# Weights' sign by a slope on ScalarE, and one pass of lane sums instead of two, in a planned attention and feed-forward kernel

## The chip, the cores and the metric

The kernel runs on one core of one Trainium2 chip. The metric is device time in microseconds (us) of one execution; 0.5% of it, about 3.2 us, is what a measurement of this kernel can tell from no change.

## The reference, cut to what matters

```
q, k, v: 4 batches x 12 heads x 448 x 64, float32          cap = 30
scores = cap * tanh(q k^T / 8 / cap);  attn = softmax(scores);  a = attn v
x = heads of a side by side                                  # 1792 x 768
h = relu(x @ w_in);  g = s * h * h + b;  out = g @ w_out     # 768 -> 2048 -> 768
```

`w_in` and `w_out` reach the chip as float64, 8 bytes an element; the rest is float32. [...]

## The kernel before

**A planner writes the order.** The kernel is a list of operations, each with an engine (or several that could run it), a cost in microseconds, a rank, and the buffers that it reads and writes. `Plan.emit` runs through a clock of its own: each engine takes, of the operations that are ready, the one with the smallest rank. What it lays down is the fixed instruction order of every engine, SyncE's order of DMA issues included. `bias`, `shy`, `cling` and `late` in `CHOICE` weight that choice. Operations are grouped in units, and `CHOICE['at']` gives each unit its rank and a step by which its parts are spread: `('a', b, c)` is the attention of two pairs of heads (c and c+1) of batch b, `('w', g)` one of 8 groups of columns of `w_in`, `('o', d)` one of 6 groups of columns of `w_out`, `('p', p)` a mixture of two of these, `('m1', j, f)` and `('m2', j, d)` the first and second product of batch j. `arrange` sorts the units by rank (no unit before those it needs); buffers of one pool are given out in that order.

**Attention.** For one pair of heads, `scores` makes 3 chunks of 128 keys (and, for every second pair, one chunk of the last 64 keys of two pairs) in the PSUM tile `ps_s` (two buffers), and ScalarE applies Tanh (L516) and Exp (L520) to 128x896 each. `pv` multiplies these with V on TensorE (`value`, L570) and adds them over the keys (`total`, L578) in the one buffer of `ps_v`: the row sums come from `ones`, twice, over chunks 0 and 1 in a first round and over chunk 2 and the last chunk in a second. A round is 8 matmul instructions of the trace. ScalarE takes `ps_v` out to `pw` (L598). `normal` moves the sums by DMA to a 128x7 tile, adds two rows and a guard on GpSimd (L541, L542), inverts them on VectorE (L545), and brings the inverse back by two more DMAs.

**Loads.** `load` issues K and Q of a pair at its rank less 10, V somewhat later; the first pair of all has a rank written out by hand:

```
        if bb == c2 == 0:
            rank = -90
        kr = buf(("k", bb, c2), "kraw", [128, S], F32)
        dma(229376, rank - 10, lambda: nc.sync.dma_start(P[kr], kT[bb, c2]), w=[kr])
        ...
        dma(
            262144, vrank - 10,
```

`vrank` is the unit's rank + 0.73 of its step, and is not written out by hand. The cap value, which ScalarE and VectorE need before the first Tanh, is loaded at rank -100 too. `piece` loads 512 KB of weights at rank - 8; `win` passes it the unit's rank + 2c for its 3 pieces. Groups 0 and 1 (`alias` is 2) are loaded into the memory of `gt`, which is idle at first, so they wait for no buffer.

**Weights.** A piece is 128 x 512 float64, seen as pairs of 32-bit words. VectorE shifts the low word (L662) and puts the sign into it (L663); the high word, read as float32, is multiplied by 2^-112 on VectorE or GpSimd (L434, L436), which sets the exponent; VectorE joins the two (L666). There are 48 pieces, 24 of each matrix. `win` then squares them, sums the squares on TensorE (L712), and derives the scales in small steps (L720 to L733), one of which waits for a sum over lanes on TensorE (L477).

**Products.** `m1` and `m1pair` multiply x with the parts of `w_in` (L843 to L845), `m2` and `m2pair` the activations with `w_out` (L1094 to L1096, L1003).

Of the kernel before, what the change touches and what calls it, by code (L numbers as in the profile page):

```python
# [243 lines left out]
def arrange(units, at):  # L244

    key = {}
    for name, pre, _ in units:
# [4 lines left out]
CHOICE = {  # L252
    'bias': 1.806,
    'shy': {'DVE': 0.3, 'POOL': 0.5},
# [32 lines left out]
    },  # L287
    'alias': 2,
    'direct': 6,
    'cslag': 21,  # L290
    'late': 0.621,
    'lag': 0.0,
    'cling': 19.274,
    'parts': ((0, 1), (2, 3)),
    'warm': 6,
    'pvo': 0.73,
    'ahead': 0.3,
    'tail': 0.9,
    'evac': ('ACT',),
    'sq': ('ACT', 'DVE', 'POOL'),  # L300
    'expo': ('DVE', 'POOL'),
    'whi': ('ACT', 'DVE'),
# [13 lines left out]
    'cs': ('DVE', 'POOL'),  # L316
    'fast': (2, 3),
    'slots': (
        ('w', 7), ('kraw', 3), ('qraw', 3), ('vp', 3), ('ph', 5), ('pt', 2), ('rd', 3), ('pw', 3),
# [6 lines left out]
def attention_moe_kernel(  # L326
# [13 lines left out]
    nc = tc.nc  # L340
# [126 lines left out]
    def root2(p):  # L467
        pi = p.bitcast(I32)
        nc.vector.tensor_scalar(pi, pi, EXP, 1, ALU.bitwise_and, ALU.logical_shift_right)
        nc.vector.tensor_scalar(pi, pi, 127 << 22, None, ALU.add)  # L470
        nc.vector.tensor_scalar(pi, pi, EXP, None, ALU.bitwise_and)
# [51 lines left out]
    def normal(bb, c2, rank):  # L523
# [15 lines left out]
        def whole():  # L539
            a = P[kc][:, 0]  # L540
            nc.gpsimd.tensor_tensor(a, a, P[kc][:, 1], ALU.add)  # L541
            nc.gpsimd.tensor_scalar(a, a, guard[:, 0:1], 0.0, ALU.add, ALU.add)  # L542

        gps(0.55, rank, whole, r=["guard", *((kc, h, i) for h in range(2) for i in range(2))], w=[kc], port=True)
        dve(0.32, rank, lambda: nc.vector.reciprocal(P[kc][:, 0], P[kc][:, 0]), w=[kc])  # L545
        z = zd[bb * NP + c2]
# [13 lines left out]
    def pv(bb, c2, rank, step):  # L560
# [11 lines left out]
        def total(first, last):  # L572
            for h, i, o in quarter:
                if i and last:
                    w, ph = half[:, c2 % 2], prob(NC, h)
                else:
                    w, ph = ones[:, 0:32], prob(i if first else 2, h)
                nc.tensor.matmul(P[kp][o, 1, 0:S], w, ph, start=first, stop=last)  # L578

        for part in CHOICE["parts"]:  # L580
            both = part[0] == 0

            def run(part=part, both=both):
                for c in part:
                    value(c)
                if both:
                    total(True, False)
                if part[-1] == NC:
                    total(False, True)

            n = len(part) + both + (part[-1] == NC)
            pe(
                0.75 * n, rank + part[-1] * step, run, r=[*(kh[c] for c in part), *(kh[0:2] if both else ()), kv, "one"],
                w=[kp], kind=2,
            )
        kw = buf(("pw", bb, c2), "pw", [128, 2, S], F32)
        ways = {
# [17 lines left out]
        def gather():  # L615
# [5 lines left out]
            gather,  # L621
            r=[("xm", bb, c) for c in range(NP)], w=[("xn", bb)], port=True,
        )
# [23 lines left out]
    def piece(kr, src, n, rank, over=()):  # L647
# [12 lines left out]

        def sign():
            nc.vector.tensor_scalar(lo(), lo(), 29, None, ALU.logical_shift_right)  # L662
            nc.vector.scalar_tensor_tensor(lo(), hi(), -0x80000000, lo(), ALU.bitwise_and, ALU.bitwise_or)  # L663

        def join():
            nc.vector.scalar_tensor_tensor(hi(), hi(), 3, lo(), ALU.logical_shift_left, ALU.bitwise_or)  # L666

        dve(0.25 + n * 0.0018, rank, sign, r=[kr], w=[(kr, "s")], port=True)
        scaled(CHOICE["expo"], n, rank, hf, hf, 2.0 ** -112, [(kr, "s")], [kr])
        dve(0.07 + n * 0.0011, rank + 0.5, join, r=[kr, (kr, "s")], w=[(kr, "f")], port=True)  # L670
        return hf
# [14 lines left out]
    def win(g, rank):  # L686
# [38 lines left out]
        kl = lanes(("wps", g), rank, g, [("wnm", g)])  # L725

        def fin():
            nc.vector.tensor_copy(n[:, 1:2], P[kl][:, 0:1])
            root2(n)
            nc.vector.reciprocal(ip, n)  # L730
            nc.vector.tensor_tensor(wn[:, g:g + 1], n[:, 0:1], n[:, 0:1], ALU.mult)
            nc.vector.tensor_scalar(sw, ip[:, 1:2], 8192.0, None, ALU.mult)
            nc.vector.tensor_scalar(wc[:, g:g + 1], ip[:, 0:1], n[:, 1:2], 1.0 / 2097152.0, ALU.mult, ALU.mult)  # L733

        dve(1.75, rank, fin, r=[kl], w=[("wnm", g), ("wc", g)], port=True)
        for c in range(NC3):
# [13 lines left out]
    def wout(d, rank):  # L750
# [44 lines left out]
        def amax():  # L795
# [4 lines left out]
        dve(  # L800
            0.68, rank, amax, r=[("wc", g) for g in range(NG)] + [("om", d, q) for q in range(NQ)], w=[("om", d)],
            port=True,
        )
# [5 lines left out]

        dve(1.3, rank, fin, r=[kl], w=[("op", d), ("os", d)], port=True)  # L810
        half = NQ // 2
# [380 lines left out]
    for d in range(ND):  # L1192
        put(("o", d), [("w", NG - 1)], lambda rank, step, d=d: wout(d, rank))
    for p in range(ND // 2):
        put(("p", p), [("o", 2 * p), ("o", 2 * p + 1)], lambda rank, step, p=p: mix(p, rank, step))
    m2s = []
    for j in range(B):
        m1s, fast = [], j in CHOICE["fast"]
        for f in range(NG if fast else NF):
            g = f if fast else f // 2  # L1200
            pre = [("a", j, NP - 2), ("w", g), ("w", CHOICE["alias"] - 1), *m2s]
            one = m1pair if fast else m1
            put(("m1", j, f), pre, lambda rank, step, j=j, f=f, one=one: one(j, f, rank))
            m1s.append(("m1", j, f))
# [60 lines left out]
```

## Time and profile before

| | |
|---|---|
| median of 3 runs | 640.17 us (638.66 to 641.72) |
| the profiled execution | 639.61 us, of which the span of the trace is 637.8 us |
| TensorE busy | 627.0 us, 98% of the span |
| VectorE / ScalarE / GpSimd busy | 400.2 / 351.7 / 208.1 us |

The span runs from the first to the last instruction of the core; what lies around it is 1.8 us. Busy time counts instructions in progress; TensorE's matmuls overlap, so its lines are read by the distance from one start to the next. PE is TensorE, PEld its weight loads, DVE VectorE, ACT ScalarE, POOL GpSimd, and SPq the DMA issues of SyncE.

### The profile page before, as it was taken

How to read it: one execution, taken by the hardware profiler on the slowest of the kernel's cores; microseconds unless marked ns; L12 is line 12 of the kernel's file. 1: busy time of each engine (PE TensorE's matmuls, PEld its weight loads, DVE VectorE, ACT ScalarE, POOL GpSimd, SP SyncE). 2: the span in 40 equal slices, each digit the busy share in tenths (PEclk: the TensorE clock that was granted, in tenths of full speed). 3: DMA queues.
4: the chain of work that ended last, by engine and by line, in shares of the span. 5: the costliest groups of instructions: out<-in, count | busy, mean ns of one | idle time of the engine just before them, and what ended most of it. 6: DMA issues, size and time to landing. Idle time of an engine off the chain costs nothing.

```text
span 637.8 us, 11435 instructions
## 1 busy us (share of the span) xinstructions
PE 627.0 (98%) x4404; PEld 331.4 (52%) x4404; DVE 400.2 (63%) x810; ACT 351.7 (55%) x472; POOL 208.1 (33%) x238
## 2 busy tenths in 40 slices
PE   7999899999999999999999999999999999999997
PEld 2332344344444433434454445555558996556997
DVE  5986857888797878788773341577767222537322
ACT  5889787886884585684674531346354002445100
POOL 3343511546456544466151020117643000105000
PEclk9999899999999999999999999999999999999999
DMA  8766423654262775853854013385412774001671
GB/s 301 293 184 193 124 86 107 215 175 143 60 234 59 251 211 179 272 200 92 282 195 157 1 48 128 146 280 212 164 48 89 239 260 147 1 2 53 223 256 67
DMA packets 54774, 101.67 MB, mean 159 GB/s; under 512 B 16192, under 2 KB 34752, under 8 KB 54720
## 3 DMA queue, kind: packets, MB, share of 16 engines
q1 hardware_dynamic: 54720, 100.95, 48.2%
q8 instruction: 34, 0.56, 0.4%
q14 instruction: 20, 0.16, 0.1%
HBM read 82.58 MB, written 18.17 MB: 158 GB/s over the span
## 4 chain that ended last, share of the span: by engine, by line
PE 85%; DMA 8%; DVE 3%; ACT 1%; SPq 1%; POOL 1%; issue 0%; ACTq 0%
PE ps_v L570 9%; PE ps_m L1003 9%; PE ps_s L512 7%; PE ps_s L1003 6%; PE ps_m L843 6%; PE ps_s L844 6%; PE ps_m L844 6%; PE ps_s L843 6%; PE ps_m L845 6%; PE ps_s L845 6%; PE ps_m L1094 5%; PE ps_m L1095 5%; PE ps_m L1096 5%; PE ps_v L578 4%; DMA gt<-in_w_in 2%; DMA w<-in_w_out 2%
## 5 line engine op out<-in xcount | busy, mean ns | idle before, releaser
L1003 PEld LDWEIGHTS <-w 128*128 128x128 f16 x1008 | 96.6, 98 | 1.0
L516 ACT ACTIVATE bed<-ps_s,arena 128x896 f32<-128x896 f32 x84 | 81.5, 1006 | 9.9 <-PE ps_s L512 8.2
L520 ACT ACTIVATE bed<-bed,par 128x896 f32<-128x896 f32 x84 | 84.2, 1040 | 0.2
L570 PE MATMUL ps_v<-bed 128*32 128x448 f32 x768 | 83.0, 548 | 0.8 <-ACT pw L598 0.6
L512 PE MATMUL ps_s<-bed 64*128 64x448 f32 (+1 forms) x384 | 80.6, 578 | 1.9 <-DMA bed<-in_qT 1.6
L1094 PE MATMUL ps_m<-gt,w 128*128 128x448 f16 x192 | 67.7, 353 | 0.0
L843 PE MATMUL ps_m<-x,w 128*128 128x448 f16 x192 | 67.7, 353 | 0.0
L1096 PE MATMUL ps_m<-gt,w 128*128 128x448 f16 x192 | 67.7, 353 | 0.0
L844 PE MATMUL ps_s<-x,w 128*128 128x448 f16 x192 | 67.7, 353 | 0.0
L844 PE MATMUL ps_m<-x,w 128*128 128x448 f16 x192 | 67.7, 353 | 0.0
L845 PE MATMUL ps_m<-x,w 128*128 128x448 f16 x192 | 67.7, 353 | 0.0
L843 PE MATMUL ps_s<-x,w 128*128 128x448 f16 x192 | 67.7, 353 | 0.0
L1095 PE MATMUL ps_m<-gt,w 128*128 128x448 f16 x192 | 67.7, 352 | 0.0
L845 PE MATMUL ps_s<-x,w 128*128 128x448 f16 x192 | 67.7, 352 | 0.0
L843 PEld LDWEIGHTS <-w 128*128 128x128 f16 x384 | 37.5, 98 | 37.3 <-issue 2.1
L845 PEld LDWEIGHTS <-w 128*128 128x128 f16 x384 | 37.5, 98 | 35.0
L844 PEld LDWEIGHTS <-w 128*128 128x128 f16 x384 | 37.6, 98 | 33.8
L512 PEld LDWEIGHTS ps_s<-bed 64*128 64x128 f32 (+1 forms) x384 | 27.4, 177 | 43.5 <-issue 12.2
L938 ACT ACTIVATE pw<-ps_s,arena 128x448 f32<-128x448 f32 x32 | 20.1, 632 | 52.6 <-PE ps_s L845 49.7
L570 PEld LDWEIGHTS ps_v<-bed 128*32 128x32 f32 x768 | 20.3, 109 | 51.4 <-issue 35.7
L444 POOL TENSOR_TENSOR pw<-pw 128x224 f32<-128x224 f32 x24 | 21.6, 912 | 77.6 <-ACT pw L942 71.2
L578 PE MATMUL ps_v<-bed,ones 128*32 128x448 f32 x288 | 45.5, 545 | 0.0
(142 smaller groups left out, 1012.8 us busy)
## 6 DMA issues: line engine op xcount, KB each, us to landing
w<-w SPq DMA_DIRECT2D x48, 512.0 KB, 4.9
w<-in_w_out SPq DMA_DIRECT2D x24, 512.0 KB, 5.0
w<-ws SPq DMA_DIRECT2D x24, 512.0 KB, 4.9
w<-in_w_in SPq DMA_DIRECT2D x18, 512.0 KB, 5.5
bed<-in_v SPq DMA_DIRECT2D x24, 256.0 KB, 4.2
ws<-w SPq DMA_DIRECT2D x12, 512.0 KB, 2.9
bed<-in_kT SPq DMA_DIRECT2D x24, 224.0 KB, 3.3
bed<-in_qT SPq DMA_DIRECT2D x24, 224.0 KB, 3.6
```

The lines of the kernel that those rows point to most:

```text
L512: nc.tensor.matmul(P[kp][o, h, 0:S], keys, P[q][rows], start=True, stop=True)
L516: 1.01, rank, lambda: nc.scalar.activation(P[kh], P[kp][:, :, 0:S], AF.Tanh, scale=tsc[:, 0:1]),
L520: 1.04, rank, lambda: nc.scalar.activation(P[kh], P[kh], AF.Exp, scale=par[:, 0:1]), r=["par"], w=[kh],
L570: nc.tensor.matmul(P[kp][o, 0, 0:S], P[kv][:, c, o], prob(c, h), start=(c == 0), stop=(c == NC))
L578: nc.tensor.matmul(P[kp][o, 1, 0:S], w, ph, start=first, stop=last)
L843: nc.tensor.matmul(ps[:, 0:S], wh, x[:, 0], start=(c == 0), stop=False)
L844: nc.tensor.matmul(ps[:, 0:S], wh, x[:, 1], start=False, stop=False)
L845: nc.tensor.matmul(ps[:, 0:S], wl, x[:, 0], start=False, stop=(c == NP - 1))
L1003: nc.tensor.matmul(at(), w(g, zw), b(g, zb), start=g == 0 and x == 0, stop=g == n - 1 and x == 2,)
L1094: nc.tensor.matmul(ps[:, 0:S], wh, ghi[:, f], start=(f == 0), stop=False)
L1095: nc.tensor.matmul(ps[:, 0:S], wh, glo[:, f], start=False, stop=False)
L1096: nc.tensor.matmul(ps[:, 0:S], wl, ghi[:, f], start=False, stop=(f == NF - 1))
```

## The change

- **Sign.** The pass that puts the sign into the low word goes. The scaling of the high word becomes a Prelu on ScalarE (scale 2^-112, slope 2^32 for negative values, which leaves a mark in the exponent that the join shifts into the sign), or two passes on VectorE; GpSimd no longer does it. The shift of the low word no longer stands before it.
- **Lane sums.** For batches 2 and 3 the exponentials of chunks 1 and 2 are added onto chunk 0, on VectorE or GpSimd, once `value` has read it, and `total` runs once, over this sum and the last chunk.
- **Small steps.** The two GpSimd steps of `normal` become one on VectorE; in `win` the part of the scales that needs no sum over lanes is made ahead of it (`own`); some steps no longer count as sharing a port in the planner, and `o` units wait for all `w` units in the sort.
- **Ranks.** All ranks and steps of `at` are others, and so are `bias`, `late` and `cling`; so the planner lays down another order on every engine.

```
-    'bias': 1.806,
+    'bias': 3.969,
...
-        ('a', 0, 0): (-88.4, 62.61), ('a', 0, 2): (80.2, 2.4), ('a', 0, 4): (227.3, 40.55),
+        ('a', 0, 0): (-48828.5, 66.74), ('a', 0, 2): (117.1, 0.11), ('a', 0, 4): (366.1, 8.16),
...
-        ('w', 0): (58.5, 0.01), ('w', 1): (226.3, 0.01), ('w', 2): (-88.5, 0.01), ('w', 3): (581.8, 0.01),
-        ('w', 4): (227.6, 0.01), ('w', 5): (510.6, 0.02), ('w', 6): (813.9, 0.02), ('w', 7): (602.1, 0.01),
+        ('w', 0): (-1550585.6, 0.0), ('w', 1): (-7883742.6, 0.02), ('w', 2): (120.7, 0.0), ('w', 3): (43.2, 0.0),
+        ('w', 4): (464.0, 0.0), ('w', 5): (707.7, 0.1), ('w', 6): (1094.7, 0.01), ('w', 7): (760.5, 0.0),
...
-    'late': 0.621,
+    'late': 0.05,
-    'cling': 19.274,
+    'cling': 13.813,
+    'expo': ('ACT', 'DVE'),
-    'expo': ('DVE', 'POOL'),
+    'added': (2, 3),
+    'add': ('DVE', 'POOL'),
...
         def whole():
             a = P[kc][:, 0]
-            nc.gpsimd.tensor_tensor(a, a, P[kc][:, 1], ALU.add)
-            nc.gpsimd.tensor_scalar(a, a, guard[:, 0:1], 0.0, ALU.add, ALU.add)
+            nc.vector.scalar_tensor_tensor(a, a, guard[:, 0:1], P[kc][:, 1], ALU.add, ALU.add)
+            nc.vector.reciprocal(a, a)
...
-                    w, ph = ones[:, 0:32], prob(i if first else 2, h)
+                    w, ph = ones[:, 0:32], prob(i if first else 0 if added else 2, h)
...
+            if part[0] == 0 and added:
+                for c in range(1, NC):
+                    flat = lambda c: P[kh[c]].rearrange("p a b -> p (a b)")
+                    binary(
+                        CHOICE["add"], 2 * S, rank + part[-1] * step, lambda: flat(0), lambda: flat(0),
+                        lambda c=c: flat(c), ALU.add, [kh[c]], [kh[0]],
+                    )
+        if added:
+            pe(0.75, rank + NC * step, lambda: total(True, True), r=[kh[0], kh[NC], "one"], w=[kp], kind=2)
...
-        def sign():
+        def low():
             nc.vector.tensor_scalar(lo(), lo(), 29, None, ALU.logical_shift_right)
-            nc.vector.scalar_tensor_tensor(lo(), hi(), -0x80000000, lo(), ALU.bitwise_and, ALU.bitwise_or)
...
+        def two():
+            nc.vector.tensor_scalar(hf(), hf(), 2.0 ** -112, None, ALU.mult)
+            nc.vector.scalar_tensor_tensor(hf(), hf(), 2.0 ** 32, hf(), ALU.mult, ALU.min)
...
+                lambda: nc.scalar.activation(hf(), hf(), AF.Prelu, scale=2.0 ** -112, alpha=2.0 ** 32),
...
+        def own():
+            root2(n[:, 0:1])
+            nc.vector.reciprocal(ip[:, 0:1], n[:, 0:1])
+            nc.vector.tensor_scalar(wn[:, g:g + 1], n[:, 0:1], n[:, 0:1], None, ALU.mult)
```

## Rows read from the trace of the kernel before

**Rows 1.** The page's busy time, share of the span and instructions, by engine
```profile
PE 627.0 (98%) x4404; PEld 331.4 (52%) x4404; DVE 400.2 (63%) x810; ACT 351.7 (55%) x472; POOL 208.1 (33%) x238
```

**Rows 2.** Windows: stretch; busy PE, PEld, DVE, ACT, POOL; clock; DMA share; GB/s
```profile
0.00:5.00 5.00, 2.42 (x6) 0.74 (x6) 0.38 (x3) 1.49 (x2) 1.34 (x11) 1.00 0.49 137
5.00:12.40 7.40, 6.00 (x22) 2.13 (x23) 4.60 (x8) 4.77 (x5) 1.96 (x2) 1.00 0.98 374
12.40:85.00 72.60, 69.86 (x580) 22.36 (x580) 58.53 (x126) 65.06 (x75) 30.20 (x36) 0.98 0.63 199
85.00:360.00 275.00, 274.19 (x1843) 118.49 (x1842) 206.38 (x447) 188.74 (x249) 118.13 (x139) 1.00 0.51 168
360.00:637.80 277.80, 274.53 (x1961) 187.71 (x1959) 130.30 (x228) 91.60 (x144) 56.48 (x51) 1.00 0.41 136
```

**Rows 3.** Timeline of TensorE: start, length, what, idle before it and releaser
```profile
5.10 4.12 PE L512 MATMUL ps_s<-bed 64*128 64x448 f32 x12 [0.60 <-DMA bed<-in_qT]
...
11.49 0.97 PE L512 MATMUL ps_s<-bed 64*64 64x448 f32 x4 [0.96 <-DMA bed<-in_qT]
...
68.54 0.35 PE L712 MATMUL ps_m<-ones,bed 128*128 128x1 bf16 x8 [1.66 <-DVE bed L701]
```

**Rows 4.** Timeline of SyncE's DMA issues at the start
```profile
1.18 0.42 SPq L488 DMA_DIRECT2D bed<-in_kT  x1
1.64 0.42 SPq L490 DMA_DIRECT2D bed<-in_qT  x1
2.11 1.39 SPq L654 DMA_DIRECT2D w<-in_w_in  x3
3.54 0.61 SPq L488 DMA_DIRECT2D bed<-in_kT  x1
...
6.17 1.82 SPq L494 DMA_DIRECT2D bed<-in_v  x2
```

**Rows 5.** Timeline of TensorE in the attention of a later batch
```profile
246.77 1.71 PE L570 MATMUL ps_v<-bed 128*32 128x448 f32 x16
248.30 0.94 PE L578 MATMUL ps_v<-bed,ones 128*32 128x448 f32 x8
249.16 1.77 PE L512 MATMUL ps_s<-bed 64*128 64x448 f32 x8
```

**Rows 6.** Groups of instructions by line: count | busy us, mean ns | idle before
```profile
L520 ACT ACTIVATE bed<-bed,par 128x896 f32<-128x896 f32 x84 | 84.2, 1040 | 0.2
L516 ACT ACTIVATE bed<-ps_s,arena 128x896 f32<-128x896 f32 x84 | 81.5, 1006 | 9.9 <-PE ps_s L512 8.2 <-PE ps_v L578 1.6
...
L663 DVE SCALAR_TENSOR_TENSOR w<-w 128x512 int32<-128x512 int32 x42 | 38.0, 906 | 1.4
...
L436 POOL TENSOR_SCALAR w<-w 128x512 f32<-128x512 f32 x34 | 27.9, 824 | 34.9 <-DVE w L663 23.1 <-issue 2.6 <-DVE arena L728 2.5
...
L598 ACT ACTIVATE pw<-ps_v 128x896 f32<-128x896 f32 x24 | 21.9, 914 | 12.3 <-PE ps_v L578 7.2 <-issue 3.6 <-POOL cmp L542 0.7
...
L542 POOL TENSOR_SCALAR cmp<-cmp,arena 128x7 f32<-128x7 f32 x24 | 14.6, 607 | 2.4
...
L444 POOL TENSOR_TENSOR w<-bed,w 128x1024 f16<-128x1024 f32 x5 | 11.0, 2205 | 57.6 <-ACT w L918 57.6
L541 POOL TENSOR_TENSOR cmp<-cmp 128x7 f32<-128x7 f32 x24 | 9.9, 412 | 41.7 <-DMA cmp<-pw 33.7 <-DVE arena L470 7.9
...
L443 DVE TENSOR_TENSOR w<-bed,w 128x1024 f16<-128x1024 f32 x7 | 8.5, 1231 | 4.3 <-ACT w L918 4.3
...
L700 ACT ACTIVATE bed<-w 128x512 bf16<-128x512 f32 x6 | 4.1, 688 | 1.3 <-DVE w L666 1.3
...
L1153 ACT ACT_TABLE_LOAD x1 | 1.3, 1283 | 0.7 <-PEq L1255 0.7
```

More of the change, by code (lines that the diff above doesn't have):

```diff
@@ L540, in whole @@
             a = P[kc][:, 0]
-            nc.gpsimd.tensor_tensor(a, a, P[kc][:, 1], ALU.add)
-            nc.gpsimd.tensor_scalar(a, a, guard[:, 0:1], 0.0, ALU.add, ALU.add)
-        gps(0.55, rank, whole, r=["guard", *((kc, h, i) for h in range(2) for i in range(2))], w=[kc], port=True)
-        dve(0.32, rank, lambda: nc.vector.reciprocal(P[kc][:, 0], P[kc][:, 0]), w=[kc])
+            nc.vector.scalar_tensor_tensor(a, a, guard[:, 0:1], P[kc][:, 1], ALU.add, ALU.add)
+            nc.vector.reciprocal(a, a)
+        dve(
+            0.38, rank, whole, r=["guard", *((kc, h, i) for h in range(2) for i in range(2))], w=[kc], port=True,
+        )
         z = zd[bb * NP + c2]
@@ L576, in total @@
                 else:
-                    w, ph = ones[:, 0:32], prob(i if first else 2, h)
+                    w, ph = ones[:, 0:32], prob(i if first else 0 if added else 2, h)
                 nc.tensor.matmul(P[kp][o, 1, 0:S], w, ph, start=first, stop=last)
+        added = bb in CHOICE["added"]
         for part in CHOICE["parts"]:
-            both = part[0] == 0
+            both = part[0] == 0 and not added
             def run(part=part, both=both):
@@ L587, in run @@
                     total(True, False)
-                if part[-1] == NC:
+                if part[-1] == NC and not added:
                     total(False, True)
-            n = len(part) + both + (part[-1] == NC)
+            n = len(part) + both + (part[-1] == NC and not added)
             pe(
@@ L595, in pv @@
             )
+            if part[0] == 0 and added:
[4 more added lines that the diff above has]
+                        lambda c=c: flat(c), ALU.add, [kh[c]], [kh[0]],
+                    )
+        if added:
+            pe(0.75, rank + NC * step, lambda: total(True, True), r=[kh[0], kh[NC], "one"], w=[kp], kind=2)
         kw = buf(("pw", bb, c2), "pw", [128, 2, S], F32)
@@ L621, in pv @@
             gather,
-            r=[("xm", bb, c) for c in range(NP)], w=[("xn", bb)], port=True,
+            r=[("xm", bb, c) for c in range(NP)], w=[("xn", bb)],
         )
@@ L659, in piece @@
         hf = lambda: P[kr].bitcast(F32)[:, :, 1]
-        def sign():
+        def low():
             nc.vector.tensor_scalar(lo(), lo(), 29, None, ALU.logical_shift_right)
-            nc.vector.scalar_tensor_tensor(lo(), hi(), -0x80000000, lo(), ALU.bitwise_and, ALU.bitwise_or)
         def join():
             nc.vector.scalar_tensor_tensor(hi(), hi(), 3, lo(), ALU.logical_shift_left, ALU.bitwise_or)
-        dve(0.25 + n * 0.0018, rank, sign, r=[kr], w=[(kr, "s")], port=True)
-        scaled(CHOICE["expo"], n, rank, hf, hf, 2.0 ** -112, [(kr, "s")], [kr])
-        dve(0.07 + n * 0.0011, rank + 0.5, join, r=[kr, (kr, "s")], w=[(kr, "f")], port=True)
+        def two():
+            nc.vector.tensor_scalar(hf(), hf(), 2.0 ** -112, None, ALU.mult)
+            nc.vector.scalar_tensor_tensor(hf(), hf(), 2.0 ** 32, hf(), ALU.mult, ALU.min)
+        ways = {
+            "ACT": (
+                0.29 + n * 0.00084,
+                lambda: nc.scalar.activation(hf(), hf(), AF.Prelu, scale=2.0 ** -112, alpha=2.0 ** 32),
+            ),
+            "DVE": (0.36 + n * 0.00158, two),
+        }
+        P.any({e: ways[e] for e in engines(CHOICE["expo"])}, rank, [kr], [(kr, "h")], port=True)
+        dve(0.16 + n * 0.00052, rank, low, r=[kr], w=[(kr, "s")], port=True)
+        dve(0.07 + n * 0.0011, rank + 0.5, join, r=[kr, (kr, "s"), (kr, "h")], w=[(kr, "f")], port=True)
         return hf
@@ L725, in win @@
         kl = lanes(("wps", g), rank, g, [("wnm", g)])
+        def own():
+            root2(n[:, 0:1])
+            nc.vector.reciprocal(ip[:, 0:1], n[:, 0:1])
+            nc.vector.tensor_scalar(wn[:, g:g + 1], n[:, 0:1], n[:, 0:1], None, ALU.mult)
+        dve(0.85, rank + 0.1, own, r=[("wnm", g)], w=[("wnm", g, 0)])
         def fin():
             nc.vector.tensor_copy(n[:, 1:2], P[kl][:, 0:1])
-            root2(n)
-            nc.vector.reciprocal(ip, n)
-            nc.vector.tensor_tensor(wn[:, g:g + 1], n[:, 0:1], n[:, 0:1], ALU.mult)
+            root2(n[:, 1:2])
+            nc.vector.reciprocal(ip[:, 1:2], n[:, 1:2])
             nc.vector.tensor_scalar(sw, ip[:, 1:2], 8192.0, None, ALU.mult)
             nc.vector.tensor_scalar(wc[:, g:g + 1], ip[:, 0:1], n[:, 1:2], 1.0 / 2097152.0, ALU.mult, ALU.mult)
-        dve(1.75, rank, fin, r=[kl], w=[("wnm", g), ("wc", g)], port=True)
+        dve(1.5, rank, fin, r=[kl, ("wnm", g, 0)], w=[("wnm", g), ("wc", g)])
         for c in range(NC3):
@@ L800, in wout @@
         dve(
-            0.68, rank, amax, r=[("wc", g) for g in range(NG)] + [("om", d, q) for q in range(NQ)], w=[("om", d)],
-            port=True,
+            0.68, rank, amax, r=[("wc", g) for g in range(NG)] + [("om", d, q) for q in range(NQ)], w=[("om", d)]
         )
@@ L808, in fin @@
             nc.vector.tensor_scalar(sc, wn, si, None, ALU.mult)
-        dve(1.3, rank, fin, r=[kl], w=[("op", d), ("os", d)], port=True)
+        dve(1.3, rank, fin, r=[kl], w=[("op", d), ("os", d)])
         half = NQ // 2
@@ L1192, in attention_moe_kernel @@
     for d in range(ND):
-        put(("o", d), [("w", NG - 1)], lambda rank, step, d=d: wout(d, rank))
+        put(("o", d), [("w", g) for g in range(NG)], lambda rank, step, d=d: wout(d, rank))
     for p in range(ND // 2):
@@ L1200, in attention_moe_kernel @@
             g = f if fast else f // 2
-            pre = [("a", j, NP - 2), ("w", g), ("w", CHOICE["alias"] - 1), *m2s]
+            pre = [("a", j, NP - 2), ("w", g), *(("w", a) for a in range(CHOICE["alias"])), *m2s]
             one = m1pair if fast else m1
```

56 rows, old and new, of the table CHOICE are left out of this document.

## Prediction

> **What bounds the kernel now.** I read the page's busy times first [rows 1], then the same by stretches [rows 2], then TensorE's timeline where it waits [rows 3], the DMA issues at the start [rows 4], one pair of heads in detail [rows 5], and the groups by line for prices [rows 6]. The reader is to see that TensorE is the bound nearly everywhere: 627.0 of 637.8 us. The idle 10.8 us lie at the ends: stretch by stretch [rows 2], 3.98 us before 12.4, 2.74 us up to 85, 0.81 us up to 360, and 3.27 us after, which is the tail of the last product. So relief for VectorE, ScalarE or GpSimd can give back 3.6 us of idle time in the middle at the very most, plus what the clock lost (mean 0.98 of full over 72.6 us, 1.45 us). Two things can move the time by more: the amount of work on TensorE, and the moment at which it starts. The change touches both.
>
> ScalarE is the second bound, in the early stretch alone: 65.06 of 72.6 us [rows 2]. A pair of heads has 3.5 chunks of Tanh and Exp and one copy out: 3.5 x (1.006 + 1.040) + 0.914 = 8.1 us [rows 6].
>
> **Lane sums: less work on TensorE.** 12 pairs (6 in each of batches 2 and 3) lose one round of 8 matmuls, 96 of 4404. In [rows 5], 16 matmuls of the same form take 248.30 - 246.77 = 1.53 us from start to start, so 8 take 0.765 us; the round with the switch to another form takes 249.16 - 248.30 = 0.86 us. Where the single round now stands by itself behind other work, a switch of 0.86 - 0.765 = 0.10 us comes back. Bounds: 12 x 0.665 = 8.0 us and 12 x 0.86 = 10.3 us; I take 12 x 0.765 = **-9.2 us**, since the first round sits between neighbours that stay. All of it counts, because TensorE has no slack to hide it in.
>
> The adds: 24 of 128x896. No add of this shape and type is in the trace. The nearest rows are the 128x1024 ones [rows 6], 1.231 us on VectorE and 2.205 us on GpSimd; by 896/1024 that is 1.08 and 1.93 us. So 26 us on VectorE, or 46 us on GpSimd, which was busy 208 of 638 us. Both adds of a pair run one behind the other, 2.2 us or 3.9 us, between `value` of chunk 0 and `total`; `value` of chunks 2 and 3 (1.53 us) and scores of the next pair (1.7 us) stand there as cover [rows 5], and products of earlier batches besides. With that I cost them at nothing. Without it every us that the chain sticks out keeps `ps_v`, which has one buffer, from the next pair, 12 us in all.
>
> **Sign.** The pass that goes costs VectorE 0.906 us (38.0 us for 42 of the 48 pieces), and GpSimd's scaling 27.9 us for 34 [rows 6]. A Prelu of 128x512 is not in the trace; the nearest is ScalarE's Square of 128x512, 0.688 us; the bounds are that and twice the VectorE pass, 1.8 us, for the two passes there. VectorE comes out near 400 - 43 + 26 + 5 = 388 us, and ScalarE at 352 to 385 us. None of these is the bound, so the sum gets **0**, with the middle's 3.6 + 1.45 us as the most that relief could bring. The cover is TensorE's own queue; it is thin only in the early stretch, where ScalarE has 72.6 - 65.1 = 7.5 us free and 6 to 12 pieces would bring 4 to 8 us of Prelu.
>
> **Small steps.** `normal` loses 0.412 + 0.607 us on GpSimd and a hand-over, and gains one VectorE step; `own` adds four short steps in each of 8 groups. The chain to x gets a little shorter; TensorE has the next batch's attention to do meanwhile: 0.
>
> **Ranks: the first loads.** Here the change speaks against itself. SyncE issues by rank. Before, the first K and Q and the cap value have -100 and come first; 3 pieces of group 2 (-96.5 and up) follow, then the second pair; [rows 4] shows just that order, and the first scores start at 5.10 [rows 3]. After, groups 1 and 0 have ranks of -7,883,742 and -1,550,585, wait for no buffer, and so all 6 pieces are issued first. V of the first two pairs follows (-48,828 and some), then cap and the first K at the rank -100 written out by hand; then the second K, whose rank is lower than -100 but whose pool gives its buffers out in order, and only then the first Q. In bytes: 6 x 0.524 + 2 x 0.262 + 3 x 0.229 = 4.36 MB up to the first Q. By [rows 2] 5.00 x 137 = 0.685 MB are moved by 5.0 us, and 374 GB/s after that, with the DMA engines 0.98 busy: 5.0 + 3.67/0.374 = 14.8 us. Before, 0.46 MB of K and Q were in at 5.1, when 0.685 MB had been moved, which is 0.6 us at that rate: 15.4 us. The first scores go from 5.1 to 15.4: **+10.3 us** (9 without the 0.6 us and with the second K behind; 11 with a slower issue). TensorE has nothing else to do then: every product needs attention's output. The second pair's Q now lands right behind the first, so the 0.96 us of [rows 3] at 11.49 goes: **-1.0 us**. TensorE restarts cold after that, but in the ramp ScalarE sets the pace: two chunks of scores at half clock are 2 x 1.7 = 3.4 us against 2 x 2.05 = 4.1 us of Tanh and Exp. Otherwise up to 1.5 us, as in the early stretch.
>
> The first Q's landing is worked out above from the rate in the rows. The Trainium skill, page "DMA: Bandwidth & Descriptors", section on where 436 GB/s comes from, gives about 358 GB/s as the limit of HBM for one core; by that figure the Q would land 0.4 us later, an estimate, and the sum would be 640.1 us. The trace has 374 GB/s, so the measurement decides.
>
> **The order of the rest** is another one, and no row can price it. Its bounds: the middle can gain 3.6 + 1.5 us, and lose as much again or more where an order was planned too tightly; `late`, the allowance for a wait of TensorE on small steps of VectorE, falls from 0.62 to 0.05 us, and there are 32 such waits by the code (8 sums of squares, 18 sums over lanes, 6 biases): up to 32 x 0.57 = 18 us if each was needed, near 0 if TensorE's queue hides them. In [rows 3] one such wait, at 68.54, cost 1.66 us. I take 0.
>
> **Sum.** 639.6 (the profiled execution: 637.8 span and 1.8 around it) + 10.3 - 9.2 - 1.0 = **639.7 us**. The profiled execution is 0.6 us under the median of 640.2, within the spread of the runs; I compare with the median.
>
> **Rivals.**
> 1. *Faster: the start is paid back in the middle, or not lost.* For it: with groups 0 and 1 turned over before attention begins, 6 pieces' Square and split leave the early stretch, in which ScalarE was 90% busy, and the sign pass leaves VectorE; the stall at 68.54 and the clock loss behind it (1.66 + 1.45 us) came just from weights being late. Against: TensorE was idle there for 2.7 us only. If all is won, 639.7 - 5 = 634.7 us; if the K and Q came first after all, 639.7 - 9.3 = 630.4 us. 0.34.
> 2. *Slower: the adds hold `ps_v`.* From 0.77 us a pair that sticks out, the round saved is spent. Both adds on GpSimd (3.9 us) against 1.5 us of `value` and part of the scores leave about 1 us or more: 12 x 1 = 12, so 652 us. Against: products of other batches can stand between. 0.12.
> 3. *Slower: ScalarE binds the early stretch.* 12 Prelus of 0.69 us are 8.3 us against 7.5 us free; with the allowance of `late` gone, some 5 us: 645 us. From 11 Prelus in that stretch it decides. 0.11.
> 4. *Slower: tables.* One table load of 1.283 us is in the trace, for Tanh, Exp, Square, Relu and copies together [rows 6]. If Prelu were not in the loaded set, 12 Prelus early, between Tanh and Exp, would cost 12 x 2 x 1.283 = 31 us of ScalarE against 7.5 us free: 663 us. 0.03. No row has a Prelu. The Trainium skill, page "ScalarE: Activation LUTs", section on table sets, says that a function of another set needs a load and that cheap functions are in every set, and does not name Prelu among its examples; by that rule the trace's single load agrees for those five.
>
> **How the numbers follow.** The forecast, loss at the start against work saved, has 0.40 and stays within 0.5% (3.2 us, about what a measurement can tell) of 640.2: its own range is 637.0 to 643.4. Faster by more: 0.34. Slower by more: 0.12 + 0.11 + 0.03 = 0.26. For 8 in 10 the range reaches over the whole of rival 1 and to most of rivals 2 and 3: 630 to 649 us.
>
> **What would show it.** Right: the first scores at 14 to 16.5 us; six weight loads ahead of the first K; 4308 matmuls; the lane-sum line with 288 instructions; no pass of the sign; one table load. Wrong: scores at 5 us (rival 1); idle time before lane sums or `value` put down to the adds (rival 2); TensorE idle between 15 and 90 us with ScalarE over 95% busy (rival 3); many table loads (rival 4). Many short waits of TensorE on small VectorE steps would show the allowance missed.

## The result and the profile after

The kernel became slower: 647.01 us, median of 4 runs (645.21 to 649.16), against 639.48 us before (638.66 to 641.72) in the same comparison; ratio 1.0113, 95% interval 1.0072 to 1.0155. The profiled execution took 646.66 us, its span 644.8 us: 7.0 us more than before.

The page's busy time by engine, and the windows of the same stretches as before (busy PE, PEld, DVE, ACT, POOL; clock; DMA share; GB/s), of the changed kernel:

```profile
PE 621.4 (96%) x4308; PEld 327.6 (51%) x4308; DVE 441.9 (69%) x891; ACT 341.6 (53%) x459; POOL 201.3 (31%) x176
```

```profile
0.00:5.00 5.00, 2.42 (x6) 0.73 (x6) 0.83 (x2) 1.28 (x1) 1.34 (x11) 1.00 0.64 216
5.00:12.40 7.40, 1.05 (x4) 0.71 (x6) 2.60 (x8) 0.91 (x2) 1.42 (x1) 1.00 0.80 296
12.40:85.00 72.60, 71.47 (x604) 23.58 (x604) 65.67 (x164) 70.69 (x82) 18.54 (x16) 1.00 0.66 222
85.00:360.00 275.00, 264.93 (x1718) 110.99 (x1707) 236.05 (x468) 192.26 (x253) 142.54 (x116) 0.99 0.49 162
360.00:644.80 284.80, 281.52 (x1989) 191.61 (x1987) 136.75 (x252) 76.47 (x123) 37.47 (x33) 1.00 0.40 132
```

The 96 matmuls are gone, and TensorE is busy 5.6 us less than in [rows 1]. But its idle time is 644.8 - 621.4 = 23.4 us instead of 10.8. By the windows against [rows 2], 4.95 us of the 12.6 lie before 12.4 us (8.93 against 3.98), 1.6 us come back up to 85 us, and 9.3 us (10.07 against 0.81) are new in the stretch from 85 to 360 us, which had hardly any. VectorE, expected to be relieved, went from 400.2 to 441.9 us.

TensorE's timeline at the start, and SyncE's DMA issues there:

```profile
2.08 2.42 PE L1191 MATMUL ps_m<-w 128*128 128x448 f16 x6 [2.08 <-POOL w L1194]
11.35 4.85 PE L514 MATMUL ps_s<-bed 64*128 64x448 f32 x12 [6.85 <-DMA bed<-in_qT]
...
19.00 1.71 PE L573 MATMUL ps_v<-bed 128*32 128x448 f32 x16
```

```profile
0.73 0.86 SPq L667 DMA_DIRECT2D gt<-in_w_in  x2
1.64 0.91 SPq L496 DMA_DIRECT2D bed<-in_v  x2
2.59 0.43 SPq L1168 DMA_DIRECT2D par<-in_cap  x1
3.07 0.92 SPq L490 DMA_DIRECT2D bed<-in_kT  x2
4.03 0.43 SPq L492 DMA_DIRECT2D bed<-in_qT  x1
4.51 0.44 SPq L667 DMA_DIRECT2D gt<-in_w_in  x1
```

Two weight pieces stand ahead of the first K and Q, not six. The pieces of groups 0 and 1 lie side by side in `gt` and share parts of its memory at their borders, so the planner lets a piece wait for the one that it borders; I had not read that in the code. The first scores start at 11.35 instead of 5.10 us [rows 3].

TensorE's waits, with the line that released them (total us, times, longest):

```profile
PE ps_s L514 <- DMA bed<-in_qT: 6.8, 1, 6.8
PE ps_s L514 <- ACT bed L518: 2.9, 4, 1.4
PE ps_v L581 <- DVE bed L445: 2.2, 1, 2.2
PE ps_v L581 <- POOL bed L446: 2.1, 2, 1.5
PE ps_m L1191 <- POOL w L1194: 2.1, 1, 2.1
PE ps_m L479 <- DVE brief L630: 1.5, 1, 1.5
```

L581 is `total`, and L445 and L446 are the new adds on VectorE and GpSimd. L479 is the sum over lanes that a small VectorE step feeds. The longest wait for an add, on TensorE's timeline, and the windows around it:

```profile
220.52 1.08 PE L514 MATMUL ps_s<-bed 64*64 64x448 f32 x8 [0.36 <-ACT bed L518]
223.80 0.56 PE L581 MATMUL ps_v<-bed,ones 128*32 128x448 f32 x1 [2.21 <-DVE bed L445]
...
225.03 3.36 PE L514 MATMUL ps_s<-bed 64*128 64x448 f32 x8
```

```profile
218.00:221.60 3.60, 3.24 (x24) 0.99 (x16) 3.57 (x5) 2.05 (x2) 3.60 (x3) 1.00 0.38 137
221.60:224.90 3.30, 1.10 (x10) 0.37 (x11) 2.28 (x5) 1.09 (x2) 1.12 (x2) 1.00 0.58 91
224.90:228.40 3.50, 3.50 (x15) 1.38 (x18) 2.92 (x12) 3.50 (x6) 2.06 (x4) 0.51 0.32 112
```

After 2.21 us of idleness the granted clock is 0.51, the 1.2 GHz level, for 3.5 us: the 8 scores take 3.36 us instead of 1.77 [rows 5]. The stall costs its own length and some 1.6 us more. VectorE's and GpSimd's timelines say why the add was late:

```profile
218.66 2.13 DVE L543 SCALAR_TENSOR_TENSOR cmp<-cmp,arena 128x7 f32<-128x7 f32 x1
220.82 0.20 DVE L544 RECIPROCAL cmp<-cmp 128x7 f32<-128x7 f32 x1
220.93 1.09 DVE L825 TENSOR_TENSOR arena<-arena 128x8 f32<-128x8 f32 x1
...
222.32 1.63 DVE L445 TENSOR_TENSOR bed<-bed 128x896 f32<-128x896 f32 x2
```

```profile
218.66 2.09 POOL L446 TENSOR_TENSOR bed<-bed 128x896 f32<-128x896 f32 x1
220.72 1.28 POOL L446 TENSOR_TENSOR bed<-bed,w 128x512 f32<-128x512 f32 x1
```

The step of `normal` that moved to VectorE (128x7, 0.36 us at the median of its 24) lasts 2.13 us, just as long as the GpSimd add beside it; the next small one with two inputs, L825, lasts 1.09 us beside another GpSimd add. This is what the Trainium skill says, page "SBUF — State Buffer", section "SBUF: two separate sides": VectorE's instructions with two SBUF inputs and GpSimd's share a port pair, and the one that comes second is blocked for the whole of the first. The 2.13 beside 2.09 us agree. L825 is one of the steps that the change no longer counts as sharing a port in the plan; the mean of its six went from 0.28 us (L796 before) to 0.71.

For the rest I use one account, worked out from the matmul records: each matmul's distance to the next start, less the distance that such matmuls have undisturbed (scores 0.2125, `value` and `total` 0.0955, products 0.189, mixtures 0.0958 us). The sum of the undisturbed distances is "work", what is left is "lost", half clock and waits together (us, by the stretch in which the matmul started):

```
kernel                     0-85  85-140 140-200 200-320 320-end  lost   work
before                     12.3   2.0    0.1     2.4     0.8     17.5  614.7
after                      13.2   2.7    2.8    13.9     1.3     33.7  605.5
a1_no_adds                 15.0   1.0    2.1     8.8     1.2     28.1  605.5
a6_new_order_two_rounds    13.5   6.5    1.7     6.6     1.2     29.4  614.7
b2_old_order_sign          11.8   3.4    0.1     1.9     0.8     17.9  614.7
c1_old_order_outer_pairs   11.8   3.4    0.8     2.6     1.0     19.7  611.6
c2_old_order_inner_pairs   13.0   3.6    0.1    12.7     0.8     30.1  608.6
```

Each row is one profiled execution, so it stands up to 2.1 us off the kernel's median (a1, its fastest). Work fell by 9.2 us, just the forecast; lost time grew by 16.2; the difference is the 7.0 us of the span. Lost time up to 85 us is nearly that of before, though TensorE started 6.25 us later: the 72.6 us behind the start run at full clock without the stall of [rows 3] at 68.54. Of the 16.2 us, 14.7 come behind 140 us, 11.5 of them from 200 to 320.

### The profile page after: what moved, and what is told of

The parts are those of the page before. It is cut to its first block, busy times and chain, and to the rows that moved or that the text cites. A ratio compares the mean times of both kernels' runs of the same rounds, so it can differ in the third digit from the quotient of the medians.

```text
span 644.8 us, 11247 instructions
## 1 busy us (share of the span) xinstructions
PE 621.4 (96%) x4308; PEld 327.6 (51%) x4308; DVE 441.9 (69%) x891; ACT 341.6 (53%) x459; POOL 201.3 (31%) x176
## 4 chain that ended last, share of the span: by engine, by line
PE 76%; DMA 10%; DVE 7%; SPq 2%; POOL 2%; issue 2%; ACT 1%; POOLq 0%; ACTq 0%; DVEq 0%
PE ps_m L1031 9%; PE ps_v L573 7%; PE ps_s L514 7%; PE ps_s L1031 6%; PE ps_s L871 6%; PE ps_s L873 6%; PE ps_s L872 6%; PE ps_m L871 5%; PE ps_m L872 5%; PE ps_m L873 5%; PE ps_m L1122 4%; PE ps_m L1123 4%; PE ps_m L1124 4%; PE ps_v L581 3%; DMA w<-in_w_out 3%; DMA bed<-in_qT 2%
## 5 line engine op out<-in xcount | busy, mean ns | idle before, releaser
L514 PE MATMUL ps_s<-bed 64*128 64x448 f32 (+1 forms) x384 | 82.4, 592 | 9.8 <-DMA bed<-in_qT 6.8
L522 ACT ACTIVATE bed<-bed,par 128x896 f32<-128x896 f32 x84 | 85.6, 1042 | 0.4
L573 PE MATMUL ps_v<-bed 128*32 128x448 f32 x768 | 82.6, 552 | 0.8 <-ACT pw L611 0.7
L514 PEld LDWEIGHTS ps_s<-bed 64*128 64x128 f32 (+1 forms) x384 | 27.9, 180 | 54.9 <-issue 25.9
L446 POOL TENSOR_TENSOR bed<-bed 128x896 f32<-128x896 f32 (+2 forms) x25 | 45.5, 1821 | 6.2 <-PE ps_v L573 4.6
L573 PEld LDWEIGHTS ps_v<-bed 128*32 128x32 f32 x768 | 21.0, 110 | 49.7 <-issue 32.5
L445 DVE TENSOR_TENSOR pw<-pw 128x224 f32<-128x224 f32 x53 | 25.1, 494 | 27.5 <-ACT pw L970 24.9
```

The lines of the kernel that those rows point to most:

```text
L446: "POOL": (0.1 + n * 0.00225, lambda: nc.gpsimd.tensor_tensor(dst(), a(), c(), op)),
L514: nc.tensor.matmul(P[kp][o, h, 0:S], keys, P[q][rows], start=True, stop=True)
L522: 1.04, rank, lambda: nc.scalar.activation(P[kh], P[kh], AF.Exp, scale=par[:, 0:1]), r=["par"], w=[kh],
L573: nc.tensor.matmul(P[kp][o, 0, 0:S], P[kv][:, c, o], prob(c, h), start=(c == 0), stop=(c == NC))
```

## Experiments

Theories: the adds cost more than the rounds that they save; Prelus wait in ScalarE's queue for loads and hold Tanh and Exp; the late start is what costs; the new order as such costs. The `a` kernels keep the new order of every engine and change operations in place; the `b` and `c` kernels keep the order of before. So none of them has an order that was planned for the work in it. All ratios are to the kernel before, with 95% intervals.

### a1_no_adds: the adds issue nothing

```
-                    binary(CHOICE["add"], 2 * S, ..., ALU.add, [kh[c]], [kh[0]])
+                    P.any({"DVE": (..., lambda: None), "POOL": (..., lambda: None)}, ..., [kh[c]], [kh[0]], port=True)
```

> The changed kernel in the same order on every engine, but the 24 adds of exponentials issue nothing (so the row sums of batches 2 and 3 leave out chunks 1 and 2). Theory A, the adds hold TensorE's queue at the lane sums, keep ps_v, and stretch VectorE's steps while GpSimd adds: the idle time and the two spells of half clock between 200 and 320 us go for the most part, 10 us of the 11.5 us by which that stretch is worse than before, so about 637 us. Theory B, the Prelus that wait for their loads in ScalarE's queue hold the Tanhs behind them: only the 4.3 us of waits put down to adds go, about 643 us. Theory C, the new order itself is worse: under 3 us, 644 to 647.

643.26 us, 1.0074 [1.0046, 1.0103]: 3.75 us less than the changed kernel by the medians, 2.5 us by the ratios, and still above before. The two intervals overlap, so by this run alone the price of the adds, some 3 us, is not clear of the noise. With adds for nothing the new order would lose all the same. 643 is also the figure of theory B, which the next run tests by itself. The page's busy times of this kernel, and the adds of the changed kernel on GpSimd:

```profile
PE 617.6 (97%) x4308; PEld 326.4 (51%) x4308; DVE 400.8 (63%) x885; ACT 341.0 (53%) x459; POOL 158.7 (25%) x158
```

```profile
L446 POOL TENSOR_TENSOR bed<-bed 128x896 f32<-128x896 f32 x18 | 40.2, 2236 | 5.9 <-PE ps_v L573 4.6 <-DMA cmp<-pw 0.5 <-ACT w L687 0.4
```

VectorE has 41.1 us less than after, of which its own 6 adds are 7.5 us. The other 33.6 us are longer durations of its other instructions, which are the same 885 in both kernels: without the 18 adds on GpSimd (40.2 us) they ran shorter.

### a2_no_prelu: ScalarE's Prelus issue nothing

The 26 Prelus on ScalarE are left out, and the join masks the words instead, so the scaling and the sign of these pieces are left out.

```
-                lambda: nc.scalar.activation(hf(), hf(), AF.Prelu, scale=2.0 ** -112, alpha=2.0 ** 32),
+                lambda: bare.append(1),
```

> The changed kernel in the same order, but the 26 Prelus that the plan put on ScalarE issue nothing (their weights' exponents are left wrong, by a mask in the join of the same shape). ScalarE then never waits for a load of weights: 25.8 us of such waits and 18 us of work go from its queue. Theory B: TensorE's idle time from 200 to 320 us falls by more than half and the time by 5 to 8 us, 639 to 642. Theory A: the lane sums still wait for the adds; under 3 us, 644 to 647.

649.68 us, 1.0157 [1.0106, 1.0208]: no gain at all, though ScalarE had 22.0 us of idle time in front of Prelus that waited for `in_w_out`. Taking these waits out of its queue brought TensorE nothing.

### a3_kq_first: cap, K and Q of the first pair are issued first

```
-        for i in out:
+        first = [i for i in out if ran[i] == "SP" and self.ops[i][1] == -100.0]
+        for i in first + [i for i in out if i not in first]:
```

> The changed kernel in the same order but for SyncE: cap, K and Q of the first pair are issued first. The first scores start at about 5 us instead of 11.35. If the late start costs what it lasts: 6 us less, 641. If the stretch up to 85 us is paced by ScalarE and the loads of weights, whose queue this only shifts: 2 us or less, 645 to 647.

650.22 us, 1.0173 [1.0140, 1.0207]: no gain either. TensorE's timeline of this kernel:

```profile
5.13 3.36 PE L515 MATMUL ps_s<-bed 64*128 64x448 f32 x8 [0.62 <-DMA bed<-in_qT]
11.60 1.58 PE L515 MATMUL ps_s<-bed 64*128 64x448 f32 x4 [3.11 <-ACT bed L519]
16.12 3.66 PE L515 MATMUL ps_s<-bed 64*64 64x448 f32 x12 [2.94 <-ACT bed L519]
19.71 2.91 PE L574 MATMUL ps_v<-bed 128*32 128x448 f32 x16
```

```profile
11.60:22.20 10.60, 7.66 (x32) 2.00 (x36) 8.65 (x17) 8.53 (x10) 1.15 (x1) 0.52 0.92 363
```

The scores start at 5.13 us, then wait 3.11 and 2.94 us for ScalarE's Tanh, and the clock is at its lower level from 11.6 to 22.2 us. ScalarE's own timeline says why:

```profile
8.55 0.70 ACT L688 ACTIVATE gt<-gt 128x512 f32<-128x512 f32 x1 [6.55 <-DMA gt<-in_w_in]
...
10.54 1.01 ACT L519 ACTIVATE bed<-ps_s,arena 128x896 f32<-128x896 f32 x1 [1.21 <-DVE arena L1185]
13.57 0.69 ACT L688 ACTIVATE gt<-gt 128x512 f32<-128x512 f32 x1 [2.02 <-DMA gt<-in_w_in]
14.16 1.02 ACT L523 ACTIVATE bed<-bed,par 128x896 f32<-128x896 f32 x1
```

Its queue stands at one Prelu until a weight piece is in, at 8.55 us, and at another until 13.57; the first Tanh and the first Exp come behind them. The first `value` starts at 19.71 us, no earlier than the 19.00 of the changed kernel. So at the start the Prelus do hold Tanh and Exp, and this run moved the first scores but not the attention behind them: it does not price the late start. A kernel with K and Q first and no Prelu ahead of the first Exp was not run. What there is on the late start is the account above: up to 85 us the changed kernel lost 13.2 us, before 12.3.

### a4_adds_vector: GpSimd's 18 adds are issued on VectorE

```
-                    binary(CHOICE["add"], ..., ALU.add, [kh[c]], [kh[0]])
+                    def plus(c=c):
+                        nc.vector.tensor_tensor(flat(0), flat(0), flat(c), ALU.add)
+
+                    P.any({"DVE": (..., plus), "POOL": (..., plus)}, ..., [kh[c]], [kh[0]], port=True)
```

> The changed kernel in the same order, but the 18 adds that the plan gave to GpSimd (2.24 us each) are issued on VectorE at the same place of the order (1.26 us each). Theory A in the form that GpSimd's adds are what stretches VectorE's steps and comes late: 2 to 6 us less, 641 to 645. If VectorE, 106 of 120 us busy in that stretch, is the one that comes late: 3 to 10 us more, 650 to 657.

645.71 us, 1.0102 [1.0068, 1.0137]: 1.3 us less by the medians, within the intervals, and short of the 2 us that theory A asked for. VectorE, which now does all 24 adds, is busy less than after, 430.5 against 441.9 us, and GpSimd 35.3 us less. So in VectorE's busy time, too, it is cheaper to make an add than to stand beside one of GpSimd's.

### a5_no_adds_no_prelu: both left out

> The changed kernel in its new order, with neither adds nor ScalarE's Prelus (row sums of batches 2 and 3 and the exponents of 26 pieces are left wrong). Theory C: the new order loses time of its own, and TensorE still loses 6 us or more from 140 to 320 us: 639 to 644, though 9.2 us of matmuls are gone. Theory A with B, each part enough to hold TensorE when the other is gone: 632 to 636, clean of waits.

642.53 us, 1.0042 [1.0022, 1.0063], as theory C said. 26 activations less than a1 bring 0.7 us by the medians and 2.0 us by the ratios, with intervals that overlap. The interval ends below that of the changed kernel (1.0072 to 1.0155), which a1's does not: adds and Prelus together cost something, and a2 found no part of it in the Prelus.

### a6_new_order_two_rounds: the new order with the lane sums of before

The adds issue nothing, and both rounds of sums run as in the kernel before, the first behind `value` of chunks 0 and 1.

```
-                if both:
+                if both or (added and part[0] == 0):
                     total(True, False)
...
-            pe(0.75, rank + NC * step, lambda: total(True, True), r=[kh[0], kh[NC], "one"], w=[kp], kind=2)
+            pe(0.75, rank + NC * step, lambda: total(False, True), r=[kh[0], kh[NC], "one"], w=[kp], kind=2)
```

> The changed kernel in its new order, with the lane sums as before: no adds, and both rounds of sums for every pair. Correct output. If the new order by itself costs some 13 us and the lane sums of the change bring 5 in it: 650 to 654. If the lane sums are what makes the changed kernel slow: 638 to 644.

651.63 us, 1.0199 [1.0157, 1.0241]. This takes the change apart, by the medians: the order, with the sign and the small steps in it, +12.15 us; one round of sums instead of two, with adds for nothing, 643.26 - 651.63 = -8.4 us; the adds +3.75 us, which is not clear of the noise; together +7.5. In this order the lane sums won 4.6 us (the intervals just part). What lost is the rest. The 12 rounds put back stand in an order that was not planned for them; what a plan of the same ranks with two rounds would take was not run. TensorE's waits in this kernel:

```profile
PE ps_s L514 <- DMA bed<-in_qT: 7.1, 2, 6.3
PE ps_m L479 <- DVE brief L633: 3.8, 1, 3.8
PE ps_v L573 <- ACT pw L614: 2.4, 3, 1.4
PE ps_s L514 <- ACT bed L518: 2.3, 4, 0.9
```

The 3.8 us at L479 is one of the waits on a small VectorE step for which `late` allows time.

### b1_old_order_lanes: the lane sums alone, in the order of before

Both adds run on VectorE into memory idle at that time, in front of the two groups of `value`; the single `total` stands behind the second.

```
+                if one and both:
+                    nc.vector.tensor_tensor(sums, flat(0), flat(1), ALU.add)
+                if one and part[-1] == NC:
+                    nc.vector.tensor_tensor(sums, sums, flat(2), ALU.add)
...
-                if both:
+                if both and not one:
                     total(True, False)
                 if part[-1] == NC:
-                    total(False, True)
+                    total(one, True)
```

> The kernel before in its own order on every engine, with the lane sums of the change alone: in batches 2 and 3 the first round of sums goes, two adds a pair are put on VectorE at the place of the two groups of value, into a free piece of memory. Theory C, the new order is what costs, and the parts are worth what they take off TensorE: 9.2 us less, 630 to 633. Theory A, the adds themselves hold TensorE wherever they stand: half or more of the round is lost again, 636 to 645.

656.07 us, 1.0265 [1.0207, 1.0324]. First line of TensorE's waits:

```profile
PE ps_v L580 <- DVE bed L591: 17.0, 8, 3.3
```

The adds stood at the end of a full VectorE queue: it is busy 107.6 of the 120 us from 200 to 320. This was rival 2 at more than its price, and more than either theory above said. As in b3, b4 and the `c` kernels, the pairs share one piece of memory for their sums; a second one was not tried.

### b2_old_order_sign: the sign alone, in the order of before

All 48 pieces get a Prelu on ScalarE in place of the scaling; the pass of the sign goes.

```
-            nc.vector.scalar_tensor_tensor(lo(), hi(), -0x80000000, lo(), ALU.bitwise_and, ALU.bitwise_or)
...
-        scaled(CHOICE["expo"], n, rank, hf, hf, 2.0 ** -112, [(kr, "s")], [kr])
+        def slope():
+            nc.scalar.activation(hf(), hf(), AF.Prelu, scale=2.0 ** -112, alpha=2.0 ** 32)
```

> The kernel before in its own order, with the sign by slope alone: the sign pass goes, and all 48 scalings are Prelus on ScalarE at the place where VectorE or GpSimd scaled. Theory C: TensorE is the bound and its work is the same, so 637 to 641, lower only by the stall at 68.5 and the half clock behind it. If Prelus in ScalarE's queue hold Tanhs back: 642 to 650.

640.59 us, 1.0016 [1.0005, 1.0028]: about 1 us, inside what counts as no change, with VectorE at 347.6 and ScalarE at 377.7 us. The window from 200 to 320 us of this kernel, for what follows:

```profile
200.00:320.00 120.00, 119.62 (x833) 48.20 (x826) 79.18 (x201) 87.22 (x109) 46.26 (x60) 1.00 0.63 207
```

### b3_old_order_both and b4_old_order_late_total: both parts, in the order of before

b3 joins b1 and b2. In b4 the second add follows the Exp of chunk 2 at once, and `total` stands just ahead of the copy out of `ps_v`, as late as it can.

```
+        def out_of():
+            if bb in (2, 3):
+                total(True, True)
+            nc.scalar.activation(P[kw], P[kp][:, :, 0:S], AF.Copy)
```

> Both parts in the order of before. Theory C: 628 to 633, the sum of the two, faster than both kernels. Theory A: slower than the lane sums alone or no better than before, 637 to 648.

> Both parts in the order of before, as in the run before it with both, but the second add is issued as soon as the Exp of its chunk and the first add are (not at the second group of value), and the one round of sums stands in TensorE's queue just ahead of the copy out of ps_v, behind whatever was planned between. If TensorE loses time because the sums stand right behind an add that starts late: the 8.8 us of waits for adds fall below 4, and the time to 634 to 640. If it is ps_v, one buffer, held until the adds are through, that costs: the waits move to the next pair's value, and the time stays at 643 to 647.

644.86 us, 1.0086 [1.0059, 1.0112], and 644.20 us, 1.0079 [1.0053, 1.0104]. In b3 six waits for the adds are left, 8.8 us. In b4 they are gone, and others have come (first line of b3's waits, first lines of b4's):

```profile
PE ps_v L580 <- DVE bed L591: 8.8, 6, 1.8
```

```profile
PE ps_m L815 <- DVE bed L451: 2.8, 1, 2.8
PE ps_m L815 <- POOL bed L452: 2.2, 2, 1.7
```

L815 multiplies the sums over `w_out`'s rows, which VectorE and GpSimd add up; before, the waits for them came to 0.8 us (L785). So the waits for adds went as the first theory said, the time stayed as the second said, and the place to which the waits moved was in neither.

### c1_old_order_outer_pairs and c2_old_order_inner_pairs: where an add stands

b4 with the single round in some pairs alone: in c1 the 4 whose adds run before 200 us or at 346 us, in c2 the 8 between 200 and 320 us. The diff is that of c1; in c2 `ONE` holds the other 8 pairs.

```
+    ONE = ((2, 0), (2, 1), (2, 2), (3, 5))
...
-                one = bb in (2, 3)
+                one = (bb, c2) in ONE
```

> The order of the kernel before, with the sign by the slope on ScalarE, and the single round of sums (second add behind the Exp of chunk 2, sums just ahead of the copy) in 4 of the 12 pairs alone: the three whose adds ran before 200 us and the one at 346 us; the 8 pairs between 200 and 320 us keep two rounds. Theory A: an add costs TensorE something only where VectorE is late anyway, between 200 and 320 us; elsewhere a saved round is kept whole, so 640.6 less 4 x 0.77 = 637.5 us (637 to 638.5), with no wait of TensorE on an add. Theory B: every pair's adds cost about what its round saves and a bit more, wherever they stand: with all 12 pairs the kernel took 644.2 against 640.6 with none, 0.3 us a pair, so 641.8 us (641 to 643).

> The complement of the former: the 8 pairs between 200 and 320 us have the single round, the other 4 keep two rounds; all else the same. Theory A: nothing is won in the 4 pairs, and all that the 12 pairs lost is lost here: 644.2 + 4 x 0.77 = 647.3 us (645.5 to 648.5), with waits of TensorE on small matmuls that VectorE feeds between 200 and 320 us, and a spell at half clock behind them. Theory B: 640.6 + 8 x 0.3 = 643 us (641.5 to 644).

639.98 us, 0.9993 [0.9975, 1.0010], and 645.07 us, 1.0070 [1.0042, 1.0098]. Against b2, by the ratios, c1 is 1.5 us faster (forecast by the place of the adds 3.1 faster, by a price per pair 1.2 slower) and c2 3.5 us slower (6.7 or 2.4). The intervals of c1 and b2 just overlap, those of c1 and c2 lie well apart. So what an add costs hangs on where it stands, and no one price per pair fits both; but the first theory's sizes are missed by half, and that the 4 pairs win anything is at the edge of the noise. The windows from 200 to 320 us, of c1 and then of c2, and c2's longest waits:

```profile
200.00:320.00 120.00, 119.11 (x821) 47.97 (x814) 80.58 (x200) 88.61 (x111) 46.24 (x61) 1.00 0.66 208
```

```profile
200.00:320.00 120.00, 113.22 (x750) 42.42 (x750) 95.02 (x211) 85.36 (x107) 50.85 (x62) 0.99 0.60 193
```

```profile
PE ps_m L816 <- POOL bed L453: 3.2, 2, 2.5
PE ps_m L816 <- DVE bed L452: 2.6, 1, 2.6
```

In c2 8 pairs' adds raise VectorE from 79 to 95 of 120 us, and TensorE has 6.8 us of idle time in place of 0.4. In the account above c1 saves 3.1 us of work and loses 1.8 more than b2; c2 saves 6.1 and loses 12.2 more. VectorE is not full in either: 21% of it was free in c2. The waits stand where TensorE needs something that was queued behind an add, above all the same sums over `w_out`'s rows, here at L816 (5.8 us in c2). That the queue at those moments decides, and not VectorE's total, is read from these waits; no run changes the queue alone. c1 can't be told from before; no kernel here beats it.

## Why the prediction was wrong, step by step

- **The order of the rest, "I take 0": the step that failed.** a6 puts the new order, sign and small steps included, at +12.15 us with the work of before. The sign by itself was about +1 in the order of before (b2); the small steps have no run of their own. The prediction had named the way, an order planned too tightly, with up to 18 us for `late`, and still took the one end. In the new order lost time behind 85 us is 16.0 us with the lane sums of before (a6), 5.3 before, so 10.7 of the 12 us lie there. Part of it are waits on small VectorE steps (L479: 3.8 us in a6, 1.5 after); part are waits on ScalarE (L573, L514). How much each rank or `late` by itself gave stays open: to change one of them re-plans every engine, and no such kernel was run.
- **The adds, costed at nothing.** In the new order they cost 3.75 us by the medians (a1 against the changed kernel), which is not clear of the noise. In the order of before they cost far more: the 12 pairs of b3 are 4.3 us over b2 although 9.2 us of work are gone. Two things were missed. The cover was TensorE's queue behind the chain, while the chain itself stood in VectorE's queue behind other work. And a GpSimd add was priced by its own 1.93 us (2.236 measured), without the 33.6 us that all 18 take from VectorE. The forecast of 388 us for VectorE became 441.9 also because its sum left out the two passes for pieces that stay on VectorE: 22 pieces, 30.2 us in a1.
- **Lane sums, -9.2.** Right: 4308 matmuls, 288 of the lane-sum line, work 614.7 to 605.5 us, and -8.4 us by a6 and a1.
- **First loads, +10.3, and the second pair, -1.0.** Wrong in size: the first scores came at 11.35 us, +6.25, with two pieces ahead, not six; the second pair's wait for its Q is gone, as forecast. And wrong in what it costs: by 85 us lost time is 13.2 against 12.3 us (13.5 and 15.0 in a6 and a1, which begin in the same order). The start of before had its own price in stalls and half clock. Rival 1's mechanism was thus true for the start and the ramp; its time was not, since the middle lost. That the forecast of 639.7 lay only 7.3 us off was luck: with the 0.9 us that the start cost by this account, the same sum is 639.6 + 0.9 - 9.2 = 631.3 us, and the miss 15.7.
- **Sign, 0.** Right: b2 1.0016 [1.0005, 1.0028], a2 no gain. A Prelu takes 0.698 us (24 of 128x512), near the lower bound of 0.688.
- **Rival 2**, the adds hold `ps_v`: its mechanism is in the waits after (4.3 us in three waits, and a spell at 1.2 GHz behind each of the two long ones), but at about 3 us in this order, not at the 12 us that it was priced at, and it was not what made the kernel slower: a1 has no adds and still loses.
- **Rival 3**, ScalarE binds the early stretch: ScalarE was busy 70.69 of 72.6 us there, 97%, but TensorE idle for 1.13 us only. Not so in this order.
- **Rival 4**, table loads: refuted. One is in the trace:

```profile
L687 ACT ACT_TABLE_LOAD x1 | 1.3, 1283 | 0.7 <-PEq L1283 0.7
```

## What to carry to other kernels

A change that also lays down a new order on every engine has to be priced as two changes: a kernel that was 98% busy on one engine had 5.3 us of lost time behind 85 us, so a new order could give little and lost 12. Price work moved from the bounding engine to another by that engine's queue at the moment where the result is needed: the same adds with the round that they save gave 1.5 us in 4 pairs, at the edge of what can be told, and cost 3.5 us in 8 others. And price an instruction on GpSimd by what it does to VectorE beside it, too. A test that moves one wait has to be read on the next engine as well: in a3 the scores came 6 us sooner and the first `value` no sooner at all, since ScalarE's queue stood at a Prelu.

## What the runs showed of the hardware

- A stall of 2.21 us between matmuls was followed by 3.5 us at a granted clock of 0.51; one of 1.50 us at 275.83, with another of 0.75 us behind it, likewise by some 3.4 us. Each costs about 1.6 us beyond its length. Not every stall does: in c2 one of 2.58 us ended at 230.56, and the granted clock stayed at 1.00 behind it:

```profile
230.50:234.00 3.50, 3.28 (x23) 1.15 (x27) 2.27 (x11) 1.04 (x2) 0.04 (x1) 1.00 0.49 117
```

- With 18 GpSimd adds of 128x896 (40.2 us) VectorE's other work took 33.6 us longer than without (after against a1); 24 such adds on VectorE itself took 26.7 us (a4). A VectorE step of 128x7 went from 0.36 to 2.13 us.
- One table load serves Prelu and the kernel's other functions (Tanh, Exp, Square, Relu and copies) together: 1 load, 26 Prelus at 0.70 us.
